# A higher limit on the length of bursts of filler matmuls between score tiles, in a two-layer attention and mixer kernel

## The chip, the cores and the metric

The kernel runs on one core of one Trainium2 chip. The metric is the time of one execution on the device, in microseconds; lower is better. The kernel before takes 1725.9 us (median of three runs, 1723.1 to 1727.19). A change counts as faster or slower when it moves the time by over 2%.

Engine names are those of the profile: PE is TensorE (matmuls), PEld its weight loads, ACT the Activation engine, DVE VectorE, POOL GpSimd, SP the engine that issues the transfers.

## The reference

The reference applies two blocks in turn, twice, with the same weights both times:

```python
# x: (1, 2048, 640) bf16;  H = 32 heads of 20
def _A_ref(x, wqkv, wo):                  # attention
    qkv = (x @ wqkv).reshape(B, S, 3, H, Dh) ...
    scores = einsum("bhqd,bhkd->bhqk", q, k) * Dh ** -0.5
    p = softmax(scores)
    o = einsum("bhqk,bhkd->bhqd", p, v)
    return o.transpose(...).reshape(B, S, D) @ wo

def _B_ref(x, w1, b1, w2, b2):            # mixer over the 2048 tokens
    h = layernorm(x)
    u = gelu(einsum("bsd,sf->bdf", h, w1) + b1)     # F = 1536
    return (einsum("bdf,fs->bds", u, w2) + b2).transpose(0, 2, 1)

x = x + _A_ref(layernorm(x), A_wqkv, A_wo)
x = x + _B_ref(layernorm(x), B_w1, B_b1, B_w2, B_b2)
# ... and both again
```

What costs time is the softmax: 2 layers x 32 heads x 2048 x 2048 exponentials.

## The kernel before

The program is written by a list scheduler that runs when the kernel is built. It keeps a guessed clock for each engine and always emits the work that can start first; the hardware then runs the resulting fixed order, each engine in its own order. The parts that matter here:

- A *score unit* is 4 heads x 128 keys x 512 queries. Its four matmuls contract over 32 rows each and sit in four row strips of the array ("row" mode). TensorE fills score tiles of three and of two banks in turn, and the Activation engine takes the exponential of each (tile `P`, from L887).
- Some units go to VectorE instead, as many as the scheduler thinks it can finish in time. VectorE evicts four banks (tile `JT`, L840) and makes the exponential of five passes of integer arithmetic (L860).
- The weighted sums (L927), the projections and mixer matmuls (L456) and the output projection (L1066) use four column strips ("col" mode). The L456 and L1066 groups are *fills*: they run between score tiles. One fill matmul is emitted as four column strips, which run at the same time; I call these four a group.
- When TensorE would idle in attention and has had little to do in the last 3.4 us, the scheduler inserts padding: a multiplication by a zero matrix (L1488).

```python
PE_MM = 216.0          # guess for a matmul group of 512 columns; 136.0 for 320 columns
SW = 100.0             # guess for a change between row and col mode
FILL_OVER = 0.0
FILL_NS = 400.0        # longest burst of one fill
DMA_RATE = 400.0       # guess: bytes per ns

def do_fill(start, f, n):            # n is FILL_NS
    ...
    t = start
    state.col = fill_mode(f) == "col"
    while t - start < n:
        # the guard: leave off when the next score tile (s_at) could start
        if t > start and t + f["cost"] + (SW if state.col or f["bf16"] else 0.0) > s_at[0] + FILL_OVER:
            break
        if f["mm_ready"] and f["mm_ready"][f["idx"]] > t + 300:
            break
        f["mms"][f["idx"]](f["tile"])
        hist.append((t, f["cost"] / 216.0))
        t += f["cost"]
        f["idx"] += 1
        if f["idx"] == len(f["mms"]):
            ...                      # group done: evict, free the bank
            break
    clk["PE"] = t
```

The mixer's first product is done in three parts as its rows become ready. The second part reads `w1` in twelve blocks of 128 KB through two buffers (tile `W`), adds a stored partial sum (`uacca`), and stores the result (`uacc`). The last 512 rows of `w1` (four transfers of 384 KB) go into key tiles (`KT`) as soon as attention no longer needs those; they are first read after the end of attention.

```python
def load_w1(ft):                       # one block, when one of two buffers is free
    dma(tl, B_w1[rows of this part, ft * 128:(ft + 1) * 128], ..., rate=DMA_RATE * 0.6, ...)

def keys_dead(g, upto):                # called when a group of heads has made its last scores
    ...
        if g == -(-NL * F // S) - 1:
            load_w1l()

def load_w1l():
    for sti in range(NL):              # NL = 4 transfers of 384 KB
        dma(tl[:, sti, :], B_w1[(NS_ + sti) * 128:(NS_ + sti + 1) * 128, :], 128 * F * 2, ...)
```

The softmax here doesn't subtract the row's maximum and nothing guards it: scores larger than these inputs give would overflow.

## Time and profile before

| | before |
|---|---|
| span of the profiled run | 1722.5 us |
| last exponential of layer 0 / layer 1 (timeline) | 797.9 / 1648.2 us |
| Activation engine idle within attention, layer 0 / layer 1 | 20.3 / 26.1 us |
| TensorE at half clock between 100 and 1650 us | 10.2 us |

The first fence is part 1 of the profile's page: busy time, share of the span, instructions.

```profile
span 1722.5 us, 50500 instructions
PE 1646.1 (96%) x21916; PEld 641.2 (37%) x21917; DVE 1464.6 (85%) x2630; ACT 1581.0 (92%) x1427; POOL 167.5 (10%) x261
```

The second is the table of stretches of time: for each stretch its length, then the busy time and instruction count of each engine, the granted clock and the transfers' share and rate.

```profile
core 0: us, PE busy (x) PEld busy (x) DVE busy (x) ACT busy (x) POOL busy (x), PEclk, DMA share, GB/s
150.00:800.00 650.00, 624.07 (x8254) 216.66 (x8246) 616.71 (x1074) 640.49 (x565) 62.02 (x83) 0.99 0.16 49
800.00:1000.00 200.00, 193.60 (x3045) 101.75 (x3046) 99.61 (x209) 158.32 (x162) 18.88 (x41) 1.00 0.24 76
1000.00:1650.00 650.00, 622.46 (x8238) 219.12 (x8235) 608.03 (x1061) 641.57 (x565) 60.39 (x84) 1.00 0.19 58
```

In both attention stages the Activation engine is busy 640 and 642 of 650 us: exponentials bound them. VectorE carries nearly as much; TensorE looks full, but part of its work is padding. The third fence shows groups of instructions by form: count, busy time, mean ns of one, then idle time of the engine before them and what ended it.

```profile
L887 ACT ACTIVATE P<-pst 128x1536 bf16<-128x1536 f32 x667 | 1014.8, 1521 | 21.1 <-PE pst L700 11.5 <-PE pst L927 7.6
L887 ACT ACTIVATE P<-pst 128x1024 bf16<-128x1024 f32 x667 | 734.6, 1102 | 5.8 <-PE pst L700 3.0 <-PE pst L927 2.1
L860 DVE TENSOR_SCALAR JT<-JT 128x2048 uint16<-128x2048 uint16 x950 | 636.4, 701 | 5.0 <-PE pst L927 1.8 <-PE pst L456 0.6
L840 DVE TENSOR_SCALAR JT<-pst 128x512 uint16<-128x512 f32 x760 | 507.4, 679 | 63.9 <-PE pst L700 61.5
```

All 1335 exponentials together are preceded by 27 us of idle. That is the most that fewer waits for TensorE could win in attention. The change aims at the mode switches; in the timeline of TensorE (start, duration, operation, count) they look like this:

```profile
402.20 0.39 PE L700 MATMUL pst<-QT,KT 32*128 32x512 bf16 x2
402.52 0.40 PE L927 MATMUL pst<-P,Vaug 128*32 128x512 bf16 x4
402.89 0.40 PE L927 MATMUL pst<-JT,Vaug 128*32 128x512 bf16 x4
403.46 0.40 PE L700 MATMUL pst<-QT,KT 32*128 32x512 bf16 x4 [0.17 <-ACT P L887]
403.79 0.40 PE L927 MATMUL pst<-P,Vaug 128*32 128x512 bf16 x3
```

From a score tile (L700) to a weighted sum (L927) the starts lie 0.32 and 0.33 us apart. Over the whole trace the median is 322 ns with a switch and 216 to 226 ns between two col groups of 512 columns.

### The profile page before, as it was taken

To read this page: it belongs to the slowest core of one execution; us is meant where nothing else is said; L and a number is where in the kernel's file an instruction comes from. 1 tells how busy PE (TensorE), PEld (TensorE's weight loads), DVE (VectorE), ACT (ScalarE), POOL (GpSimd) and SP (SyncE) were. 2 spreads that over 40 slices of the span, in tenths; PEclk is the share of its full clock that TensorE was granted. 3 is DMA by queue.
4 is the path that set the end of the run, shared out by engine and by line. 5 is a ranking of instruction groups with operands and counts; after the bars stand their busy time and mean duration, and the time that the engine had idled before them with its cause. 6 is when DMAs were issued, how large, how long until landed. Compare 5 with 4: busy or idle time off the path is not lost. (4 is left out here: it accounts for less than half of the span.)

```text
span 1722.5 us, 50500 instructions
## 1 busy us (share of the span) xinstructions
PE 1646.1 (96%) x21916; PEld 641.2 (37%) x21917; DVE 1464.6 (85%) x2630; ACT 1581.0 (92%) x1427; POOL 167.5 (10%) x261
## 2 busy tenths in 40 slices
PE   8999999999999999998999999999999999998989
PEld 3433333332333333335545432333333333332356
DVE  6688999999989999999444489999999888999963
ACT  7899999999999999997598899999999999999950
POOL 3100002000200020001100000110011000200010
PEclk9999999999999999999999999999999999999999
DMA  3200001000112106511422000100002120257143
GB/s 119 29 2 2 2 13 36 2 1 2 52 57 71 39 32 190 182 34 43 148 84 75 25 2 2 33 32 1 1 17 58 57 70 32 76 179 216 42 125 95
DMA packets 103295, 98.06 MB, mean 57 GB/s; under 512 B 45600, under 2 KB 79520, under 8 KB 103072
## 3 DMA queue, kind: packets, MB, share of 16 engines
q1 hardware_dynamic: 99456, 94.82, 17.8%
q8 instruction: 171, 2.80, 0.7%
q0 software_dynamic: 3616, 0.01, 0.3%
q14 instruction: 52, 0.43, 0.1%
HBM read 63.35 MB, written 31.46 MB: 55 GB/s over the span
## 5 line engine op out<-in xcount | busy, mean ns | idle before, releaser
L887 ACT ACTIVATE P<-pst 128x1536 bf16<-128x1536 f32 (+1 forms) x1335 | 1520.2, 1311 | 26.9 <-PE pst L700 14.5
L860 DVE TENSOR_SCALAR JT<-JT 128x2048 uint16<-128x2048 uint16 x950 | 636.4, 701 | 5.0 <-PE pst L927 1.8
L700 PE MATMUL pst<-QT,KT 32*128 32x512 bf16 (+1 forms) x4224 | 575.2, 377 | 40.7 <-ACT P L887 28.5
L840 DVE TENSOR_SCALAR JT<-pst 128x512 uint16<-128x512 f32 x760 | 507.4, 679 | 63.9 <-PE pst L700 61.5
L927 PE MATMUL pst<-P,Vaug 128*32 128x512 bf16 (+1 forms) x3440 | 500.6, 380 | 3.4 <-DVE T_85 L977 1.8
L927 PE MATMUL pst<-JT,Vaug 128*32 128x512 bf16 (+1 forms) x3920 | 465.7, 380 | 3.4 <-DVE T_85 L977 2.4
L700 PEld LDWEIGHTS <-KT 32*128 32x128 bf16 x4224 | 168.5, 91 | 512.2 <-issue 498.5
L927 PEld LDWEIGHTS <-Vaug 128*32 128x32 bf16 x7360 | 170.2, 94 | 297.3 <-issue 268.0
L1002 POOL TENSOR_TENSOR T_86<-T_85,rden 128x512 bf16<-128x512 f32 x64 | 67.5, 1054 | 1130.6 <-DVE rden L989 1090.8
L1066 PE MATMUL pst<-wo,attnT 128*32 128x320 bf16 x2048 | 111.3, 301 | 4.7 <-DVE attnT L1012 3.2
L456 PEld LDWEIGHTS <-W 128*32 128x32 bf16 x3384 | 89.7, 96 | 60.0 <-issue 28.8
L1488 PE MATMUL pst<-ident,zw 128*32 128x512 bf16 (+1 forms) x330 | 108.8, 380 | 0.0
L456 PE MATMUL pst<-hh,wq 128*32 128x512 bf16 x1232 | 104.3, 382 | 1.3 <-DVE JT L840 0.7
L456 PE MATMUL pst<-hh,wk 128*32 128x512 bf16 x1240 | 97.3, 381 | 1.1 <-DVE JT L840 0.6
L456 PE MATMUL pst<-x1last,W 128*32 128x320 bf16 x1536 | 80.6, 301 | 0.9 <-DVE JT L840 0.5
L1066 PEld LDWEIGHTS <-attnT 128*32 128x32 bf16 x2048 | 52.4, 96 | 42.2 <-issue 20.3
L456 PE MATMUL pst<-attnT,hh 128*32 128x320 bf16 x1196 | 60.2, 300 | 2.1 <-DVE hh L463 0.7
L463 DVE CAST KT<-pst 128x512 bf16<-128x512 f32 x53 | 36.0, 680 | 19.5 <-PE pst L456 18.3
L456 PE MATMUL pst<-JT,W 128*32 128x320 bf16 x1080 | 52.3, 300 | 0.0
L977 DVE STREAM_TRANSPOSE T_85<-pst 128x512 f32<-128x512 f32 (+1 forms) x58 | 40.0, 690 | 8.1 <-PE pst L927 8.0
L354 POOL TENSOR_SCALAR rt<-mv 128x1 f32<-128x1 f32 x64 | 13.4, 209 | 340.2 <-DVE mv L346 339.6
L463 DVE CAST Vaug<-pst 128x320 bf16<-128x320 f32 x43 | 20.6, 482 | 30.4 <-PE pst L456 21.6
(91 smaller groups left out, 878.0 us busy)
## 6 DMA issues: line engine op xcount, KB each, us to landing
W<-in_B_w_dram SPq DMA_DIRECT2D x10, 768.0 KB
W<-in_B_w_dram SPq DMA_DIRECT2D x24, 256.0 KB
xs<-in_A_x_dram SPq DMA_DIRECT2D x32, 160.0 KB
x2d<-xs SPq DMA_DIRECT2D x16, 320.0 KB
xs<-x2d SPq DMA_DIRECT2D x16, 320.0 KB
x1d_69<-xs SPq DMA_DIRECT2D x12, 320.0 KB
uacca_72<-W SPq DMA_DIRECT2D x12, 320.0 KB
W<-uacca_72 SPq DMA_DIRECT2D x12, 320.0 KB
```

Source lines behind the costliest of these rows:

```text
L354: nc.gpsimd.tensor_scalar(out=rt[:], in0=mv[:, 1:2], scalar1=(1.0 + LN_EPS) if double else 1.0, scalar2=LN_EPS * LN_EPS if double else LN_ ...
L456: nc.tensor.matmul(out_[32 * c:32 * c + 32], lhsT=lhsT[:, 32 * c:32 * c + 32], rhs=rhs, start=start, stop=stop, tile_position=(0, 32 * c))
L463: nc.vector.tensor_copy(out=out_, in_=in_)
L700: pe(nc.tensor.matmul(dst, lhsT=k_, rhs=q_, start=True, stop=True, tile_position=(32 * j, 0)))
L840: nc.vector.tensor_scalar(out=c["jt"][:, j * 512:(j + 1) * 512], in0=Dt[:], scalar1=SCALE * LOG2E * 256.0, scalar2=127.0 * 256.0, op0=ALU. ...
L860: nc.vector.tensor_scalar(out=tt_[:], in0=c["jt"][:], scalar1=0.5, scalar2=TERM_C[i], op0=ALU.mult, op1=ALU.add)
L887: nc.scalar.activation(out=P[:, 0:n, :].rearrange("p a b -> p (a b)"), in_=St[:, 0:n, :].rearrange("p a b -> p (a b)"), func=ACT.Exp, scal ...
L927: pe(nc.tensor.matmul(dst, lhsT=Vaug[:, n:n + 32], rhs=ap, start=acc["cnt"][j] == 1 and not part, stop=last[j] and (half is None or part = ...
L977: nc.vector.transpose(out=T1[:], in_=src[:, 0:w])
L1002: eng.tensor_tensor(out=o_, in0=a_, in1=b_, op=ALU.mult)
L1066: nc.tensor.matmul(t[32 * c:32 * c + 32, 0:w], lhsT=q_, rhs=wo_pad[:, gg, c0:c1], start=(gi == 0), stop=(gi == len(gs) - 1), tile_position ...
L1488: pe(nc.tensor.matmul(dst[0:32, 0:128 * n], lhsT=zw[:, 0:32], rhs=ident[:].unsqueeze(1).to_broadcast([128, n, 128]), start=not inside, sto ...
```

## The change

The limit of a burst goes from 400 to 600 ns. With 216 or 136 ns for a group, a burst that nothing else ends has three full or five narrow groups instead of two or three. The intent is to change between row and col mode less often.

```diff
 PV_WAIT = 400.0
-FILL_NS = 400.0
+FILL_NS = 600.0
 COL_FILL = True
```

## The prediction

> **What bounds the kernel now.** The groups by form give one exponential 1.52 us (128x1536) or 1.10 us (128x1024), 667 of each; together they keep the Activation engine busy 1520 us. By stretches of time it is busy 640 of the 650 us from 150 to 800 us and 642 of those from 1000 to 1650 us; VectorE is 95% busy in the first. So exponentials bound both attention stages. Both engines hardly wait: 27 us of idle stand before all exponentials, 61 us before VectorE's 760 score evictions. TensorE is 96% busy, but 330 of its instructions are padding multiplications by zero, so it has slack. From 810 to 1000 us, and in the tail after 1649 us (the chain of waits: 64 us of mixer matmuls), TensorE bounds.
>
> **What the change does.** Row-tiled scores and column-tiled projections alternate. The Trainium skill, "TensorEngine Tiling (Array Packing)", Key Properties, says that changing the tiling mode drains TensorE. This trace agrees: group starts lie 216 to 226 ns apart without a switch (512 wide) or 136 ns (320 wide), about 320 and 240 ns with one: 104 ns a switch. Longer bursts avoid some. A burst still breaks off when the scheduler thinks that the next score tile could start, which limits the effect. The compiled order shows:
> - mode switches 2729 -> 2692: 37 x 0.104 = 3.8 us of TensorE saved; mixer and projection runs 658 -> 630, output projection runs 211 -> 181.
> - two more score units (190 -> 192) on VectorE: 10 passes at 0.70 us and 8 evictions at 0.68 us, +12.4 us; 8 more groups of weighted sums, +1.7 us of TensorE.
> - exponentials 1335 -> 1331, about -4 us; one more copy, +0.6 us.
> - the number of score and mixer matmuls and transfers stays; the tail is the same 480 matmuls.
>
> **How much is critical.** TensorE's net 2 us lies mostly in attention, where it is not the bound; it turns into padding or idle. Only its share from 850 to 1000 us, where the Activation engine idles 15 us, can count: under 1 us. The 3 us of exponentials count if VectorE carries its extra units without making the Activation engine wait. Against that, a burst 0.2 us longer holds up weighted sums (which free P buffers) and score tiles for VectorE, and nearly every later decision of the greedy scheduler falls differently, which shifts idle by several us either way. The kernel was tuned around the old value, so I expect this scatter to be slightly unfavourable. Estimate: -3 us from work, +3 us from waits.
>
> **Prediction:** 1726 us, 8 in 10 between 1713 and 1742. Faster by over 2%: 0.01; within: 0.96; slower: 0.03.
>
> **What would show each step.** Switches: about 37 fewer groups at 320 ns, instruction durations unchanged. Work: Activation busy down 3 us, VectorE up 12 us. Criticality: each attention stage ends within 8 us of before (about 800 and 1649 us), tail unchanged at 74 us. Waits: idle before exponentials and before VectorE's evictions within 10 us of 27 and 61 us.
>
> **What would make it wrong.** If longer bursts starve VectorE or fill the P buffers, idle before exponentials rises by tens of us and the time by 1% or more. If production before 150 us or at 850 to 1000 us is paced by mode switches, full attention starts earlier and the time falls by more than 10 us.

## The result, and the profile after

The changed kernel takes 1729.6 us (median of 4 runs, 1727.54 to 1730.85), the kernel before in the same rounds 1726.55 us (4 runs). The ratio is 1.002, with a 95% interval of 1.0002 to 1.0037: the same, by the 2% rule, and slightly slower. Here and below a ratio is the mean time of one kernel's fast runs over that of the other kernel's in the same rounds, so it is not quite the ratio of the medians.

Busy time, stretches and groups of the changed kernel:

```profile
span 1727.7 us, 50530 instructions
PE 1647.4 (95%) x21922; PEld 641.2 (37%) x21922; DVE 1477.0 (85%) x2647; ACT 1577.5 (91%) x1424; POOL 170.6 (10%) x261
```

```profile
150.00:800.00 650.00, 622.49 (x8267) 217.27 (x8267) 620.45 (x1082) 638.85 (x562) 61.88 (x81) 1.00 0.16 49
800.00:1000.00 200.00, 192.96 (x3024) 101.96 (x3024) 101.17 (x212) 156.56 (x159) 20.63 (x44) 1.00 0.24 76
1000.00:1650.00 650.00, 623.07 (x8230) 217.24 (x8226) 614.59 (x1066) 636.52 (x561) 59.05 (x79) 0.99 0.18 56
```

```profile
L887 ACT ACTIVATE P<-pst 128x1536 bf16<-128x1536 f32 x666 | 1009.1, 1515 | 29.0 <-PE pst L700 16.0 <-PE pst L927 11.4
L887 ACT ACTIVATE P<-pst 128x1024 bf16<-128x1024 f32 x665 | 727.6, 1094 | 5.2 <-PE pst L700 4.6 <-PE pst L927 0.2
L860 DVE TENSOR_SCALAR JT<-JT 128x2048 uint16<-128x2048 uint16 x960 | 647.8, 706 | 4.8 <-PE pst L927 1.8
L840 DVE TENSOR_SCALAR JT<-pst 128x512 uint16<-128x512 f32 x768 | 513.4, 680 | 58.2 <-PE pst L700 56.1
```

The work moved as the compiled order said: the Activation engine has 3.5 us less of it, VectorE 12.4 us more. The idle before exponentials rose from 27 to 34 us; in layer 1 alone it rose from 11.9 to 18.3 us. The timeline tells where the time went: the last exponential of layer 0 ends at 797.8 us (before: 797.9), that of layer 1 at 1652.4 us (before: 1648.2). So of the 5.2 us by which the two profiled runs differ, 4.2 are there at the end of layer 1's attention, and the tail after it adds 1.0 (75.3 us instead of 74.3).

Within layer 1 the longest single waits of the changed kernel are near 1544 us. The waits in the stretch from 1535 to 1560 us (engine, line, what it waited for: us in total, times, longest), first of the kernel before, then of the changed one:

```profile
PE pst L456 <- DMA W<-in_B_w_dram: 0.7, 1, 0.7
ACT P L887 <- PE pst L700: 0.2, 1, 0.2
```

```profile
ACT P L887 <- PE pst L700: 4.0, 3, 3.0
DVE JT L840 <- PE pst L700: 4.0, 2, 3.7
PE pst L456 <- DMA W<-in_B_w_dram: 2.7, 1, 2.7
```

A mixer matmul waited 2.7 us for a block of `w1`. Behind it in TensorE's queue stood the score tiles, so both the Activation engine and VectorE ran dry. The timeline of the changed kernel there, TensorE and Activation engine and then the engine that issues the transfers:

```profile
1540.98 0.38 PE L700 MATMUL pst<-QT,KT 32*128 32x512 bf16 x1
...
1544.09 0.46 PE L456 MATMUL pst<-hh,W 128*32 128x320 bf16 x4 [2.73 <-DMA W<-in_B_w_dram]
...
1544.48 0.61 PE L700 MATMUL pst<-QT,KT 32*128 32x512 bf16 x3
...
1545.20 1.45 ACT L887 ACTIVATE P<-pst 128x1536 bf16<-128x1536 f32 x1 [3.01 <-PE pst L700]
```

```profile
1532.62 1.88 SPq L276 DMA_DIRECT2D KT<-in_B_w_dram  x4
1534.59 0.38 SPq L276 DMA_DIRECT2D uacc_75<-W  x1
1536.88 0.38 SPq L276 DMA_DIRECT2D W<-in_B_w_dram  x1
```

The block was issued at 1536.88 us and released the matmul at 1544.09 us, 7.2 us later. Just before it the four transfers of 384 KB into the dead key tiles had been issued, and one store of 320 KB. In the stretch from 1532.6 to 1544.1 us the transfers moved 246 GB/s; at that rate these 1.57 MB alone take 6.4 us (an estimate from the two numbers), while the scheduler's guess of 400 bytes per ns makes 3.9 us of them. The trace's records of single packets show the order: those of the four transfers (3072 bytes each) started from 1534.2 to 1541.5 us, those of the block (256 bytes each) only from 1539.8 to 1543.5 us, although it was issued at 1536.88 us. That a later transfer queues behind an earlier one on the same queue agrees with the Trainium skill, "DMA: Bandwidth & Descriptors", section Queues, rings and completion order: on each of the transfer engines descriptors are consumed in ring order. That a waiting matmul holds back those behind it agrees with "TensorE: Matmul & The Clock Gate", Part 3, The mechanism, which calls matmuls a strict FIFO: nothing ran on TensorE in the 2.73 us.

The kernel before has the same queue of transfers: its four were issued from 1527.8 us and a `w1` block at 1531.4 us. But the matmul that reads this block started at 1538.1 us, 6.7 us after the issue, and TensorE did not wait for it. In the changed kernel TensorE was ready for its block 4.5 us after the issue (at 1541.36 us). So what the new order changed is the time that it left between the issue and the reader.

A second difference is the clock. TensorE was granted half its clock, in pieces of 3.4 or 6.8 us, for 17.1 us between 100 and 1650 us in the changed kernel's trace and for 10.2 us in that of before, and once more in the changed kernel's tail (6.8 us from 1653 us). One of these pieces starts at 1544.0 us, at the end of the wait for `w1`; the score matmuls in the timeline above take 0.61 us there and 0.38 us before the wait.

### The profile page after: what moved, and what is told of

It is laid out like the page before. It is cut to its first block, busy times and chain, and to the rows that moved or that the text cites. A ratio compares the mean times of both kernels' runs of the same rounds, so it can differ in the third digit from the quotient of the medians.

```text
span 1727.7 us, 50530 instructions
## 1 busy us (share of the span) xinstructions
PE 1647.4 (95%) x21922; PEld 641.2 (37%) x21922; DVE 1477.0 (85%) x2647; ACT 1577.5 (91%) x1424; POOL 170.6 (10%) x261
## 5 line engine op out<-in xcount | busy, mean ns | idle before, releaser
L887 ACT ACTIVATE P<-pst 128x1536 bf16<-128x1536 f32 (+1 forms) x1331 | 1517.0, 1305 | 34.2 <-PE pst L700 20.5
L860 DVE TENSOR_SCALAR JT<-JT 128x2048 uint16<-128x2048 uint16 x960 | 647.8, 706 | 4.8 <-PE pst L927 1.8
L700 PE MATMUL pst<-QT,KT 32*128 32x512 bf16 (+1 forms) x4224 | 574.1, 377 | 41.6 <-ACT P L887 30.0
L840 DVE TENSOR_SCALAR JT<-pst 128x512 uint16<-128x512 f32 x768 | 513.4, 680 | 58.2 <-PE pst L700 56.1
L700 PEld LDWEIGHTS <-KT 32*128 32x128 bf16 x4224 | 162.7, 91 | 509.4 <-issue 498.4
L463 DVE CAST QT<-pst 128x512 bf16<-128x512 f32 x58 | 39.0, 673 | 9.0 <-PE pst L456 8.6
L456 PE MATMUL pst<-hh,W 128*32 128x320 bf16 x768 | 41.6, 303 | 4.3 <-DMA W<-in_B_w_dram 3.0
```

Source lines behind the costliest of these rows:

```text
L456: nc.tensor.matmul(out_[32 * c:32 * c + 32], lhsT=lhsT[:, 32 * c:32 * c + 32], rhs=rhs, start=start, stop=stop, tile_position=(0, 32 * c))
L463: nc.vector.tensor_copy(out=out_, in_=in_)
L700: pe(nc.tensor.matmul(dst, lhsT=k_, rhs=q_, start=True, stop=True, tile_position=(32 * j, 0)))
L840: nc.vector.tensor_scalar(out=c["jt"][:, j * 512:(j + 1) * 512], in0=Dt[:], scalar1=SCALE * LOG2E * 256.0, scalar2=127.0 * 256.0, op0=ALU. ...
L860: nc.vector.tensor_scalar(out=tt_[:], in0=c["jt"][:], scalar1=0.5, scalar2=TERM_C[i], op0=ALU.mult, op1=ALU.add)
L887: nc.scalar.activation(out=P[:, 0:n, :].rearrange("p a b -> p (a b)"), in_=St[:, 0:n, :].rearrange("p a b -> p (a b)"), func=ACT.Exp, scal ...
```

## The experiments

The theories, as they stood before the first runs:

- **A**: longer bursts cost nothing by themselves. The new limit reorders the program, and the small loss comes from a few single events in layer 1 (a late `w1` transfer, and half-clock pieces).
- **B** (rival): each longer burst holds up scores and weighted sums, a cost spread over both layers.
- **C** (rival): the half-clock pieces are the loss.
- **D** (A made precise, after the first runs): the event is the `w1` block that queues behind the 1.5 MB for the key tiles.

Each kernel was run in five rounds beside the kernel before and gave a correct result. Medians of before in the three sets of runs: 1723.69 us (9 runs), 1724.78 us (11 runs) and 1726.03 us (11 runs).

| kernel | median us | ratio to before | 95% interval |
|---|---|---|---|
| 600 ns in layer 0 only | 1724.8 | 1.0006 | 0.9993 to 1.002 |
| 600 ns in layer 1 only | 1728.36 | 1.003 | 1.0017 to 1.0042 |
| 600 ns, more padding | 1732.47 | 1.0053 | 1.004 to 1.0065 |
| 400 ns, more padding | 1725.74 | 1.0012 | 1.0 to 1.0025 |
| 600 ns, key-tile transfers late | 1723.77 | 0.9991 | 0.9979 to 1.0003 |
| 400 ns, key-tile transfers late | 1726.03 | 1.0005 | 0.9993 to 1.0017 |
| 600 ns, no guard | 1730.08 | 1.0025 | 1.001 to 1.0039 |
| 400 ns, one guess changed by 1 ns | 1727.51 | 1.0012 | 0.9999 to 1.0024 |
| 400 ns, key-tile transfers later still | 1722.5 | 0.9979 | 0.9967 to 0.9991 |
| 600 ns, no guard, transfers later still | 1723.74 | 0.9991 | 0.9978 to 1.0003 |
| 400 ns, collision put in | 1729.3 | 1.0021 | 1.0009 to 1.0033 |
| 600 ns (the change) again | 1732.61 | 1.0038 | 1.0022 to 1.0054 |

### One layer at a time

The compiled orders show that these two kernels are clean halves: with the new limit in layer 0 alone, layer 1 has the old order instruction for instruction, and the other way round.

```diff
-... 120, lambda s, f=f: do_fill(s, f, FILL_NS)))
+... 120, lambda s, f=f: do_fill(s, f, 600.0 if a.layer == 0 else 400.0)))   # l0_only
+... 120, lambda s, f=f: do_fill(s, f, 600.0 if a.layer == 1 else 400.0)))   # l1_only
```

> Bursts of 600 ns in layer 0 alone. Its layer 0 has the changed kernel's instruction order and its layer 1 has the old order, instruction for instruction. Theory A (longer bursts cost nothing by themselves; the small loss comes from a few single events in layer 1: a weight transfer that lands late, and half-clock windows after lulls of TensorE): layer 0 ended at 797.8 us in the changed kernel and at 797.9 us before, so the time is that of the kernel before, ratio 0.999 to 1.001. Theory B (each longer burst holds up scores and weighted sums, a cost spread over both layers): about half of the loss, ratio about 1.001, with more idle before the exponentials of layer 0 than the 20 us of before.

> Bursts of 600 ns in layer 1 alone (order of layer 1 as in the changed kernel, layer 0 as before). Theory A: all of the loss, ratio 1.001 to 1.003, with the wait for a w1 transfer near the end of layer 1 again and idle of the Activation engine in layer 1 near 32 us instead of 26. Theory B: about half of the loss, spread.

Layer 0 alone: ratio 1.0006, not told apart from 1. Layer 1 alone: 1.003, all of the loss. In its trace the wait is back at the same place (waits from 1535 to 1560 us of the kernel with layer 1 alone):

```profile
ACT P L887 <- PE pst L700: 4.4, 2, 3.2
PE pst L456 <- DMA W<-in_B_w_dram: 3.2, 1, 3.2
```

Layer 0 alone has no such wait there. Theory B wanted half of the loss in layer 0, where the burst limit acts as much. That is not what was seen, but these two ratios do not exclude it: half of the loss would be 1.0015, and the interval of layer 0 alone reaches 1.002. The transfers below decide more.

### More padding, order frozen

```diff
+        if o[0] > now + 250 and sum(h[1] for h in hist) < 15.0 and a.want and not a.done and a.acc_open():
+            return (o[0], lambda s, f=o[3]: (extra_pad(), f(s)))   # one zero multiplication, no guessed clock moved
         return (o[0], o[3])
```

> The changed kernel's order, frozen, with one more padding multiplication by zero wherever the scheduler sees TensorE idle for over 250 ns inside an open accumulation (about 156 more in the program). Theory C (half-clock windows after lulls of TensorE make the loss): the half-clock windows between 100 and 1650 us vanish or become fewer than the 17 us of the changed kernel, the mean granted clock rises from 0.990 to 0.995, and the time falls by 2 to 4 us, to ratio about 1.000. Theory A without C: the time stays at ratio 1.002. If the padding itself delays scores, it rises.

> The same padding in the kernel before, order frozen. Theory C: at most 1 us faster, since it has only 10 us of half-clock windows between 100 and 1650 us; so the two padded kernels differ by less than the unpadded ones. If the padding costs TensorE time that matters: ratio above 1.001.

Neither became faster: the changed kernel went to 1.0053, the kernel before to 1.0012 with an interval that begins at 1.0. Its half-clock time between 100 and 1650 us fell only from 17.1 to 13.7 us: the pieces near 1462 and 1609 us are gone, but one of 6.8 us now follows the wait for `w1`, which is still there with 4.1 us. The hoped-for clock did not come either: the mean granted clock of the padded changed kernel's five runs lies between 0.987 and 0.993, not at 0.995. So the padding removed too little half clock to judge theory C. Two other traces do judge it. The changed kernel with late transfers (below) has 20.5 us of half clock between 100 and 1650 us, more than the changed kernel, and no loss; the one with 600 ns in layer 0 only has 17.1 us, and a ratio of 1.0006. Theory C falls as the main cause. Whether padding without need costs time is not settled: 1.0053 (1.004 to 1.0065) overlaps with the repeat of the unpadded kernel (1.0022 to 1.0054).

That a half-clock piece does cost something where it falls on a tight spot can be read from two kernels with the same order in layer 1. The kernel before, then the one with 600 ns in layer 0 only, at the same instructions (timeline of TensorE):

```profile
1581.06 0.40 PE L700 MATMUL pst<-QT,KT 32*128 32x512 bf16 x3 [0.92 <-ACT P L887]
1581.39 0.83 PE L927 MATMUL pst<-JT,Vaug 128*32 128x512 bf16 x12
1582.15 0.40 PE L700 MATMUL pst<-QT,KT 32*128 32x512 bf16 x4
```

```profile
1581.60 0.61 PE L700 MATMUL pst<-QT,KT 32*128 32x512 bf16 x3 [0.28 <-ACT P L887]
1582.14 1.47 PE L927 MATMUL pst<-JT,Vaug 128*32 128x512 bf16 x12
1583.55 0.61 PE L700 MATMUL pst<-QT,KT 32*128 32x512 bf16 x4
```

The second trace has half clock from 1579.4 us for 6.8 us. The twelve weighted sums take 1.47 instead of 0.83 us, and the exponential that needs the buffer they free waits 2.8 instead of 1.3 us. So one piece costs about 1.5 us at this spot. Layer 1 as a whole was not longer for it (807.3 us from its first to its last exponential, 807.8 us in the kernel before). Whether it falls there changes from run to run.

### The suspected transfers taken out of the way

The orders of all four compute engines stay exactly as they were; only the four transfers of 384 KB are issued later, behind the last `w1` block of the second mixer part.

```diff
+            if hold and hold():
+                held.append((out_, in_))          # load_w1l: hold=lambda: not L.w1_issued
+            else:
+                nc.sync.dma_start(out=out_, in_=in_)
+            if flush:                             # load_w1, second part, last block
+                flush()
+                while held:
+                    o_, i_ = held.pop(0)
+                    nc.sync.dma_start(out=o_, in_=i_)
```

> The changed kernel with the instruction order of all four compute engines frozen; only the four 384 KB transfers of w1's last rows into the dead key tiles are issued later in each layer, behind the last small w1 transfer of the second mixer group instead of among them. Theory D (a w1 block lands late because it queues behind these 1.5 MB, and TensorE, in order, holds the score tiles behind the mixer matmul that waits; this is most of the loss): no TensorE wait for a transfer over 1 us near 1544 us, idle of the Activation engine in layer 1 near 28 us instead of 32, and 3 to 4 us less than the changed kernel: ratio 0.999 to 1.001. If the loss has another cause: ratio still about 1.002 to 1.003.

> The same delay of the four transfers in the kernel before, order frozen. Theory D: only the wait of 1.4 us near 687 us (and 0.7 us near 1552 us) is there to be taken away: 1 to 2 us faster, ratio 0.999 to 1.000; then the two kernels with late transfers are within 1 to 2 us of each other, and burst length by itself is worth nothing either way. If the loss has another cause: the two stay 4 to 5 us apart.

The changed kernel with late transfers: 1723.77 us, ratio 0.9991. The loss is gone, with the bursts still long. Its trace has no wait for `w1` from 1535 to 1560 us, and the last exponential of layer 1 ends at 1648.2 us instead of 1652.4. The only idle of VectorE's evictions there is this line:

```profile
DVE JT L850 <- PE pst L710: 0.3, 1, 0.3
```

(The lines of these kernels are shifted by the edit: L850 is the old L840, L710 the old L700.)

The kernel before with late transfers did not do what I expected: 1.0005, no gain. Its trace shows why. Layer 0 ended 3.4 us earlier (794.5 us), but in layer 1 a partial sum now queued behind the moved transfers. Two lines of its waits from 1551 to 1561 us:

```profile
DVE W L1262 <- DMA W<-uacca: 3.3, 1, 3.3
ACT P L897 <- PE pst L710: 2.7, 1, 2.7
```

I had moved the collision from one small transfer to another.

The length of layer 1, from its first to its last exponential in the timeline, sorts these traces:

| kernel | bursts in layer 1 | layer 1, us |
|---|---|---|
| before | short | 807.8 |
| changed | long | 811.6 |
| changed, again | long | 813.3 |
| changed, key-tile transfers late | long | 806.4 |
| 600 ns in layer 1 only | long | 812.9 |
| before, key-tile transfers late (partial sum waits) | short | 811.7 |
| before, transfers later still (next section) | short | 808.1 |
| before, collision put in (next section) | short | 813.8 |

With a wait for a transfer of 2.7 us or more, layer 1 takes 811.6 us or longer, with short bursts as with long ones; without it 808.1 us or less, again with both.

### Later still, and the collision put in

The next kernel holds the four transfers until both the last `w1` block and the last partial sum have been issued. (In the changed kernel the first rule already gives this order of transfers.) The one after it puts the suspected cause into the kernel before.

```diff
-hold=lambda: not L.w1_issued              # the edit above
+hold=lambda: len(L.last_issued) < 2      # late2: after the last block and the last partial sum
+hold=lambda: layer == 1 and not L.w1_issued   # collide10: issued just before block 11 of 12
```

> The kernel before, compute order frozen, with the four 384 KB transfers held until the last small w1 block and the last partial sum of the second mixer group have both been issued (in late_before the last partial sum still queued behind them and VectorE waited 3.3 us for it at 1557 us). Theory D: neither the wait near 687 us nor the one at 1557 us remains, layer 0 ends near 795 us and layer 1 no later than before: 1719 to 1722 us, ratio 0.997 to 0.9985. If these waits cost nothing on the whole: 1.000.

> The suspected cause put into the kernel before: compute order frozen, and in layer 1 alone the four 384 KB transfers are issued just ahead of the eleventh of the twelve w1 blocks of the second mixer group, later than before. Theory D: a TensorE wait for w1 (or a VectorE wait for a partial sum) of 2 to 4 us appears between 1545 and 1560 us, the Activation engine waits about as long, and the kernel is 2 to 4 us slower: ratio 1.001 to 1.0025, the loss of the change without its bursts. If such a wait is made up elsewhere: ratio 1.000.

Both came out as theory D said (the wait that was put in is 4.2 us, just over the 2 to 4 expected). Without collisions the kernel before takes 1722.5 us, ratio 0.9979, and no wait of a compute engine for a transfer is left between 1535 and 1560 us, nor near 687 us; TensorE waits 1.7 us for a block of `w2` at 1653 us instead, at the start of the tail. This is the fastest kernel, the only one whose interval lies below 1. With a collision put in, the old order and the old bursts lose as much as the change did: ratio 1.0021, with these waits from 1545 to 1562 us:

```profile
ACT P L897 <- PE pst L710: 5.4, 2, 4.2
DVE W L1262 <- PE pst L466: 5.4, 1, 5.4
PE pst L466 <- DMA W<-in_B_w_dram: 4.2, 1, 4.2
```

### Bursts without the guard

The guard breaks off a burst when the next score tile could start. I counted, from the scheduler itself, what ends the bursts inside attention: with 400 ns, 441 of 1385 end at the limit, 503 at the guard, 441 with their group; with 600 ns, 150 of 1135 end at the limit, 546 at the guard, 439 with their group. The mean length goes from 1.91 to 2.32 groups. Without the guard it is 3.55.

```diff
-FILL_OVER = 0.0
+FILL_OVER = 1e9        # with FILL_NS = 600.0
```

> The changed kernel without the rule that breaks a burst off when the next score tile could start (bursts inside attention: mean length 2.32 matmul groups -> 3.55; mode switches 2692 -> 2613). Theory A/D says that this rule is what kept longer bursts harmless: without it score tiles wait up to 0.6 us, the Activation engine's idle inside attention rises by over 30 us in the two layers, and the time by 1% or more, in spite of 79 x 0.104 = 8 us of switches saved. If switches on TensorE are what matters, it is faster than the changed kernel instead.

> The kernel without the rule that breaks off bursts (mean burst 3.55 matmul groups), with the same late transfers, order frozen. If burst length by itself costs nothing and even the missing rule does not (VectorE takes over 6 more score units than before): ratio as the changed kernel with late transfers had, 0.999 +- 0.001. If long bursts do hold up the exponentials: 1.001 or more, with the Activation engine's idle before exponentials still near 40 us where the changed kernel with late transfers has less.

Expected was 1% or more; measured 1.0025, and 0.9991 with the transfers late. So the guard was not what kept long bursts harmless. The groups of the kernel without guard tell what happened:

```profile
L887 ACT ACTIVATE P<-pst 128x1536 bf16<-128x1536 f32 x663 | 991.9, 1496 | 34.1 <-PE pst L700 18.3 <-PE pst L927 12.0
L887 ACT ACTIVATE P<-pst 128x1024 bf16<-128x1024 f32 x661 | 708.7, 1072 | 7.6 <-PE pst L700 5.0 <-PE pst L927 1.9
L860 DVE TENSOR_SCALAR JT<-JT 128x2048 uint16<-128x2048 uint16 x980 | 661.0, 702 | 6.1 <-PE pst L927 3.9
```

Idle before exponentials does rise, from 27 to 42 us. But the scheduler sees the Activation engine fall behind and gives VectorE six more units than before (980 passes instead of 950), which has room for them; the Activation engine's busy time falls by 7 us (1581.0 to 1574.0). The two nearly cancel. With late transfers its idle is still 39 us, against 31 in the changed kernel with late transfers, at the same ratio. In the kernel before with transfers later still it is 25 us.

With the collisions gone, bursts of 1.91, 2.32 and 3.55 groups give 0.9979, 0.9991 and 0.9991. The intervals overlap, and the second comes from another set of runs, so a cost of about 0.1% for longer bursts is not excluded; a gain is not seen. In the traces it is no clear cost of burst length: layer 1 took 808.1, 806.4 and 809.9 us, and layer 0 (first to last exponential) 775.0, 778.7 and 775.5 us.

### Two controls

```diff
-LAT_V = 120.0
+LAT_V = 121.0          # a guess of the scheduler, in the kernel before
```

> Control for scatter: the kernel before, bursts as before, with one of the scheduler's guesses changed by next to nothing (a VectorE latency of 121 instead of 120 ns), which reorders layer 0 from its early part on and layer 1 from about there too. Theory A: any reordering moves the time by some us, up or down: ratio between 0.996 and 1.004, so the change's 1.002 is inside the scatter of reorderings. If reordering alone does nothing: 1.000 within 0.001.

> The changed kernel as it is, beside the others on this chip: ratio 1.001 to 1.003 again, and again a TensorE wait for a w1 block of about 3 us near 1544 us in its trace. If that wait came by chance in the first trace, it is gone here while the loss remains.

Changing one guess by 1 ns reorders most of the program and gave 1.0012, with an interval from 0.9999 to 1.0024. That is as large as the change's first ratio of 1.002 within the intervals, without any longer burst. Its trace has the lost time in another place: layer 1 took 807.1 us, no longer than before, but began 46.0 instead of 42.5 us after the last exponential of layer 0, with half clock for 6.8 us from 803.3 us in between. That is one trace; the cause was not tested. The changed kernel again lost: 1.0038, above the 1.001 to 1.003 expected, and its wait for `w1` in layer 1 is there once more, 3.9 us. Its runs scatter more than those of the kernel before in the same set (1728.09 to 1738.42 against 1723.69 to 1728.36 us). Its profiled run was the slowest, and there layer 0 lost as well: between 685 and 705 us the Activation engine waited 4.6 us, VectorE 3.6 us for a partial sum and TensorE 1.5 us for another `w1` block; in the first trace these waits were 0.8, 0.9 and 0.3 us. These waits are not fully fixed by the order; what decides how long a transfer takes in a given run was not tested.

## Why the prediction was right or wrong

The time was right: 1726 us predicted, 1729.6 measured, inside 1713 to 1742, and "within 2%" at 0.96. That alone says little, since the medians of all kernels (1722.5 to 1732.61 us) lie inside that range.

- **What bounds the kernel** was right. The stage ends moved with waits of the Activation engine; TensorE's savings showed nowhere. They were within 8 us of before (797.8 and 1652.4 us), but not in the slow repeat (804.4 and 1661.9 us).
- **Mode switches.** Right, and small. The old trace has 2678 steps between scores and col work, the new one 2641: 37 fewer, with the same 320 ns. TensorE's busy time went from 1646.1 to 1647.4 us, its padding stayed at 330. In this total the 3.8 us cannot be seen: by the prediction's own count 1.7 us of weighted sums were added, and the half clock was 6.9 us longer. TensorE is not the bound there.
- **Work moved.** Right: -3.5 us for the Activation engine (predicted -3), +12.4 us for VectorE (predicted +12).
- **Waits.** The size was roughly right: +7.3 us before exponentials (27 to 34; predicted within 10, +3 in the sum), and 56 us before VectorE's evictions (predicted within 10 of 61). The main cause was not. The prediction named bursts "0.2 us longer" that hold up weighted sums and score tiles, plus scatter. What made the kernel slower was one event that it did not name: a late `w1` block behind 1.5 MB of other transfers. Taking it away, in the same compute order, brought the ratio from 1.002 (1.0038 when repeated) to 0.9991, and the idle from 34.2 to 30.9 us; putting one into the kernel before gave 1.0021. In the changed kernel with late transfers, so without the event, idle is still 4.0 us more than before (30.9 against 26.9), with no single wait over 1.3 us, and the Activation engine has 4.0 us less to do (1577.0 against 1581.0 us): the predicted balance of -3 and +3 fits. Whether long bursts made those waits is not shown: before two of them that recur (1.0 us near 495 and 1298 us) no fill ran for 1.5 us. In the case without guard idle rises to 42 us, and moving units to VectorE makes up for most of it. That the total came so close to the forecast although this event was missing is partly luck.
- **The guard** "limits the effect": right for switches (2692 with it, 2613 without), wrong as a protection of the time.
- **Unfavourable scatter** because the kernel "was tuned around the old value": the one control went the same way (1.0012), which is too little to show it. What the old order had in its favour was that its mixer blocks were read after they had landed, except for 1.4 us near 687 us and 0.7 us near 1552 us. That was luck of the order: the 0.9979 without such waits in attention shows that even the old order paid for it.
- **Tail "unchanged at 74 us"**: 75.3 us. There is a half-clock piece of 6.8 us at its start; whether it made the difference was not tested.

## What to carry to other kernels

In a program whose order is fixed when it is built, a parameter that changes little work can still move the time by where it places matmuls against transfers; look for the few longest waits before explaining a small loss by the parameter itself. Issue large transfers that nobody needs soon behind the small ones that the in-order matmul queue reads next: here this was worth more than any burst length. The scheduler's guess of the transfer rate (400 bytes per ns, where 246 were measured) may have let it place the reader too early, and a lower guess may cure this without moving transfers; neither was tested. To prove such a cause, freeze the order of the compute engines and move only the transfers, once away and once into the way.

## What the Trainium skill lacked or had wrong

- "TensorEngine Tiling (Array Packing)", Key Properties, says that a change of tiling mode drains TensorE but gives no cost. Here it is about 104 ns each way at full clock (322 ns from a score tile to a weighted sum, 216 to 226 ns without a change).
- "TensorE: Matmul & The Clock Gate", Why this matters for your kernels, asks for no idle gaps over about 3 us and gives one window of idle as the reason. The same page tells of another kernel whose clock swings because TensorE pauses briefly and often, but not how short and how many these pauses are. In this trace half clock follows a stretch with such short gaps: TensorE was busy 2.0 of the 3.4 us before the piece at 1462.1 us, with no gap over 0.8 us, as the stretches of the changed kernel show:

```profile
1458.70:1462.10 3.40, 1.99 (x16) 0.84 (x14) 3.40 (x7) 3.40 (x4) 0.00 (x0) 1.00 0.00 0
1462.10:1468.90 6.80, 6.39 (x63) 1.79 (x62) 5.48 (x10) 4.66 (x5) 1.05 (x1) 0.50 0.01 2
```

- "DMA: Bandwidth & Descriptors", Queues, rings and completion order, gives the order but not what it costs a small transfer: a block of 128 KB issued 2.4 us after the last of 4 x 384 KB had been issued took 7.2 us until its reader could start, at 246 GB/s in all.
